# Turning the attention weights of eight more steps by TensorE in a fused top-k attention and feed-forward kernel

## The chip, the cores and the metric

One core of one Trainium2 chip. The metric is the device time of one execution in microseconds (us), as the median of several runs. The engines: TensorE (PE; its weight loads, PEld, overlap it), VectorE (DVE), ScalarE (ACT), GpSimd (POOL) and the queues from which transfers are issued, here nearly all on SyncE (SP). TensorE writes to PSUM, and GpSimd works on SBUF alone in this kernel.

## What is computed

The reference, cut to what matters, with q, k and v of 8 batches x 8 heads x 576 rows x 64, w_in of 512 x 2048 and w_out of 2048 x 512, all float32:

```
scores = scale * np.matmul(q, k.transpose(0, 1, 3, 2))
kth = np.partition(scores, -32, axis=-1)[..., -32:-31]
scores = np.where(scores >= kth, scores, -1000000000.0)
scores = scores - np.max(scores, axis=-1, keepdims=True)
attn = np.exp(scores)
attn = attn / (np.sum(attn, axis=-1, keepdims=True) + 1e-09)
attn_out = np.matmul(attn, v)
x = attn_out.transpose(0, 2, 1, 3).reshape(4608, 512)
h = x @ w_in
return (h - np.tanh(h)) @ w_out
```

## The kernel before

**Steps.** The attention is cut into 144 steps. A step is one pair of heads (hp, four pairs in a batch) and one block of 128 rows (qt); rows 512 to 575 of two pairs of heads make a step of their own (rem). Batch 0 has steps 0 to 17: row blocks 0, 1 and then 2 with 3. Batch 1 has steps 18 to 35: first blocks 0 and 1 of each pair of heads (steps 18 to 25, part a = 0), then blocks 2 and 3 with the two rem steps (26 to 35). Later batches are like batch 1. Two steps of one pair of heads make a pair (nq = 2); the second has `last` set.

**One step on the engines.** TensorE computes the scores of step n+1 while step n is searched (L329), ACT copies them to SBUF (L337). VectorE finds the 32 largest of every row (search, L359 to L382: minima and maxima of quarters, then rounds of MAX8 and MATCH_REPLACE8). GpSimd makes the threshold tb from them (L396), and nb (L405). In the step after, mask (L415 on ACT, L418 on GpSimd) subtracts a huge number from all scores below it, and expo (L438) takes the exponent with its row sum, from which GpSimd makes rd (L448). Two steps after the search, the weights z, 128 rows x 2 heads x 576 keys, are turned so that keys lie on partitions, as the product with v (values, L561) needs them.

**Two ways of turning.** Where the step's flag `pe` is set (in batch 0 alone), turn_pe does it: nine 128x128 transposes on TensorE into PSUM (L533), which ACT copies to et in three pieces (L536). The weights aren't divided by their sum; GpSimd spreads the reciprocals of a pair over 64 columns (spread, L477), TensorE turns these too (L571), ACT copies both results (L575, xs) and GpSimd multiplies them into x (L579). Where `pe` isn't set, VectorE takes the reciprocal of the step (L457), ACT divides the weights by the sum (divide, L464), VectorE turns z in blocks of 32x32 into zx (turn_z, L496; one buffer, of 4 x 576 columns), and after a pair the blocks go to DRAM (there, L509) and back in another order (L513) into et_main or, for rem, et_rem. ACT then copies the product to x (L581).

**Lags.** values of a pair runs `lag` steps after its last step: 2 with pe, 5 (LAG) without.

**The feed-forward.** x of two row blocks of all heads is a unit. Its 30 items are 16 products with w_in (L605; after every second one ACT takes tanh, L631, and a copy, L632, and GpSimd subtracts them, L633) and 14 products with w_out, in the seven products of Strassen's scheme for 2 x 2 blocks, with sums of g by GpSimd (sum_up, L706) and joins (L753). The combinations of w_out that the scheme needs (T1 to T4, 16 of them; combine, L675 to L684) are made by GpSimd once, one with each of the items that follow in steps 17 to 22; two are put aside in DRAM (L681, L686). A dealer (rate and deal in run) hands out items evenly: in every step it takes the smallest rate at which the work at hand lasts until the next unit is ready, which it knows from the steps' lags. A unit of 30 items that is ready at step t moves the rate of all steps before it.

**Order.** All of it is written out by hand, and every engine works in the order of the program. A step n whose step n-2 has pe issues: eight transposes of step n-2 and their two copies, mask of n-1, search of n, spread of n-2 if it is the last of its pair, scores of n+1 with their copy, the ninth transpose and its copy, threshold of n, expo of n-1, most of the dealt items, values of n-2 if it is the last, loads. Without pe, 0.4 of the items are dealt ahead of the scores of n+1; reciprocal, scaling and turning of n-2 stand within the search of n.

**Memory.** `more`, `later` (the tile named spare) and et are areas that serve several purposes in turn: parts of them hold converted weights first, then q of batch 0, rx and xs (the spread reciprocals and the copy of the products), and later T2 to T4. temps, two of the combinations on their way to DRAM, lie in `later`, where et_main is as well. zx1 is first used for weights, later for turn_z.

Of the kernel before, what the change touches and what calls it, by code (L numbers as in the profile page):

```python
# [19 lines left out]
J = 4  # L20
# [34 lines left out]
def kernel(  # L55
# [11 lines left out]
    B, H, S, D = q.shape  # L67
# [3 lines left out]
    R = S - JP  # L71
# [71 lines left out]
    sums = [et_pe[:, 1024 + 512 * i : 1536 + 512 * i].rearrange("p (m n) -> p m n", n=P) for i in range(2)]  # L143
    qT0 = [more[:, i * S : (i + 1) * S] for i in range(4)]
    vb3 = more[:, 2304:2816].rearrange("p (t c d) -> p t c d", t=2, d=D)
    rx2 = [more[:, x : x + 256].rearrange("p (i t d) -> p i t d", i=2, d=D) for x in (2816, 3072)]
    xs0 = more[:, 3328:3840].rearrange("p (a n) -> p a n", a=2)
    q_first = more[:, 3264 : 3264 + S]
    temps = [later[:, i * 512 : (i + 1) * 512].rearrange("p (m n) -> p m n", m=2) for i in range(2)]
    vb_last = later[:, 6 * S : 6 * S + 512].rearrange("p (t c d) -> p t c d", t=2, d=D)  # L150
    kept_B12 = keep.tile([P, CF // 2, 2 * P], FP32, name="kept_B12")
    kept = {x: keep.tile([P, 4, 2 * P], FP32, name=f"kept_{x}") for x in ("T2", "T4")}
# [113 lines left out]
    def load_v(b, hp):  # L266


        if hp == NHP - 1:
            x = vb_last if b else vb3  # L270
        else:
            x = kqpool.tile([P, 2, J, D], FP32, tag="vb", name="vb", bufs=3)[:]
        vb[b, hp] = x
        y = vrs[hp]
        for t in range(2):
            h, o = 2 * hp + t, t * R
            nc.sync.dma_start(
                x[:, t, :, :], v[b, h, o : o + JP, :].rearrange("(c p) d -> p c d", p=P)
            )
            o = 0 if t else JP  # L280
            nc.sync.dma_start(y[half(t), t, :], v[b, h, o : o + R, :])
# [188 lines left out]
    def spread(n):  # L470

        if steps[n].last:
            rd = rds.pop(n)
            nq = steps[n].nq
            last_rx[0] ^= 1
            rx = rxs[n] = rx2[last_rx[0]]
            nc.gpsimd.tensor_copy(  # L477
                rx[:, 0:nq], rd[:, 0:nq].unsqueeze(3).to_broadcast([P, nq, 2, D])
            )
# [38 lines left out]
    def turn_pe(n):  # L518

        g, z = steps[n], st.pop(n)["z"]  # L520
        if g.rem:
            et = et_rem
        elif g.i:
            et = ets.pop(n - 1)
        else:
            et = et_pe
        ets[n] = et
        et = tiles(et, g.nq)[:, :, :, g.i, :].rearrange("p a k j -> p k a j")
        for k0 in range(0, KC, J):
            kn = min(J, KC - k0)  # L530
            zt = zt_ps.tile([P, 512], FP32, tag="zt", name="zt")
            for k in range(kn):
                nc.tensor.transpose(  # L533
                    zt[:, k * P : (k + 1) * P], z[:, (k0 + k) * P : (k0 + k + 1) * P], ident[:]
                )
            nc.scalar.copy(  # L536
                et[:, k0 : k0 + kn],
                zt[:, 0 : kn * P].rearrange("p (k a j) -> p k a j", a=NG, j=G),
            )
            if k0:  # L540
                yield
# [5 lines left out]
    def values(n):  # L547


        g = steps[n]  # L550
        nq, u = g.nq, g.unit
        et = tiles(ets.pop(n), nq)
        w = nq * P
        av = zt_ps.tile([P, 2, N], FP32, tag="zt", name="av")
        for i in range(2 if g.rem else 1):
            cols = half(i) if g.rem else slice(0, w)
            es = et[:, 2 * i : 2 * i + 2] if g.rem else et
            hp = g.hp + i
            for c in range(J + 1):
                for t in range(2):  # L560
                    nc.tensor.matmul(  # L561
                        av[half(t), 0, cols],
                        vb[g.b, hp][:, t, c, :] if c < J else vrs[hp][:, t, :],
                        es[:, :, (J + 1) * t + c if c < J else J].rearrange("p a i j -> p a (i j)"),
                        start=(c == 0),
                        stop=(c == J),
                    )
        if g.pe:
            rx = rxs.pop(n)
            for i in range(nq):  # L570
                nc.tensor.transpose(  # L571
                    in_order(av[:, 1, 0:w], nq)[:, i], rx[:, i].rearrange("p t d -> p (t d)"), ident[:]
                )
            xs = xs0
            nc.scalar.copy(xs[:, :, 0:w], av[:, :, 0:w])  # L575

        def put(dst, order, cols):
            if g.pe:
                nc.gpsimd.tensor_tensor(dst, order(xs[:, 0, cols]), order(xs[:, 1, cols]), ALU.mult)  # L579
            else:  # L580
                nc.scalar.copy(dst, order(av[:, 0, cols]))  # L581

        if g.rem:
            for i in range(2):
                put(xt(u)[:, g.hp + i, g.col : g.col + R], lambda x: x, half(i))
        else:
            dst = xt(u)[:, g.hp, g.col : g.col + w].rearrange("p (i a j) -> p i a j", a=NG, i=nq)
            put(dst, lambda x: in_order(x, nq), slice(0, w))
        if n in done:
            work.extend(ffn(u))  # L590
# [238 lines left out]
    def plan():  # L829
        steps.clear(), done.clear()  # L830

        def block(b, qt):
            return [(slice(0, P), out[b * S + qt * P : b * S + (qt + 1) * P, :])]

        rest = None
        for b in range(B):
            if b % 4 == 0:
                rest = Unit(
                    [
                        [(half(i), out[(b + k + i) * S + JP : (b + k + i + 1) * S, :]) for i in range(2)]  # L840
                        for k in (0, 2)
                    ],
                    "xTr",
                )

            parts = [(0, 1), (2, 3)]
            if b == 0:
                parts[0:1] = [(0,), (1,)]
            for a, qts in enumerate(parts):
                unit = Unit([block(b, qt) for qt in qts], "xT")  # L850
                pe = b == 0
                unit.combines = pe and a == 1
                for hp in range(NHP):
                    for i, qt in enumerate(qts):
                        steps.append(Step(b, hp, qt, unit, 0, i, len(qts), pe, a))
                    if hp == NHP - 1:
                        done[len(steps) - 1] = unit
                    if hp % 2 and a == (0 if b == B - 1 else len(parts) - 1):
                        steps.append(Step(b, hp - 1, J, rest, b % 4 * R, pe=pe, part=a))
                        if hp == NHP - 1 and b % 4 == 3:  # L860
                            done[len(steps) - 1] = rest
        for g, after in zip(steps, steps[1:]):
            if after.pe and not after.rem and not g.pe:
                g.lag = 3
# [4 lines left out]
    def run(exact):  # L869
# [8 lines left out]
        def at(n, fn):  # L878
            todo.setdefault(n, []).append(fn)
# [8 lines left out]
        for n, b, hp, part in sorted(rows):  # L888
# [14 lines left out]
                    at(n - 3 + x, turn)  # L903
                    turned[name] = n - 3 + x
            if not part:
                at(n + 3 if b else n - 1, lambda b=b, hp=hp: load_v(b, hp))

# [191 lines left out]
```

## Time and profile before

| | us |
|---|---|
| runs, median (lowest to highest, 3 runs) | 1490.44 (1490.33 to 1492.73) |
| the profiled execution, its own time | 1491.52 |
| its span, first to last instruction | 1488.7 |
| span until the search of step 20 starts | 226.81 |
| until that of step 28 | 303.33 |
| until that of step 143, the last | 1346.52 |

Busy time, in us, in four stretches of the span (columns: stretch, length, busy time and instructions of PE, PEld, DVE, ACT and POOL, the granted TensorE clock as a share of full speed, the mean busy share of the DMA engines, GB/s):

```profile
0.00:160.00 160.00, 101.50 (x550) 70.51 (x551) 143.88 (x472) 106.27 (x198) 108.42 (x149) 0.84 0.73 239
160.00:303.33 143.33, 128.78 (x1002) 83.44 (x1002) 131.14 (x536) 104.28 (x195) 124.04 (x186) 0.98 0.35 86
303.33:1346.52 1043.19, 1001.83 (x9174) 633.39 (x9172) 1004.16 (x3870) 774.22 (x1427) 808.62 (x1177) 0.99 0.68 174
1346.52:1488.66 142.14, 135.27 (x1254) 89.50 (x1250) 12.80 (x39) 38.37 (x80) 63.74 (x62) 0.98 0.26 74
```

The first stretch loads and converts the weights. In the third, VectorE and TensorE are both above 96% busy. In the last only products are left. A transfer's time to landing and an engine's wait are listed by the profile as "who waited for whom"; a wait for several things is put down to the one that came last.

The rows of the two ways of turning (line, engine, operation, out<-in, shape, count | busy us, mean ns | idle before it, and what ended it):

```profile
L464 ACT ACTIVATE z<-z,rd 128x576 f32<-128x576 f32 x252 | 181.2, 767 | 99.9 <-DVE rd L457 99.3
...
L496 DVE STREAM_TRANSPOSE zx<-z 128x1152 f32<-128x1152 f32 x126 | 171.4, 1361 | 22.8 <-ACT z L464 18.4 <-DMA there<-zx 4.3
...
L533 PE MATMUL zt<-ident,z 128*128 128x128 f32 x162 | 34.0, 351 | 7.6 <-ACT z L438 7.1 <-ACT more L575 0.5
...
L536 ACT COPY et<-zt 128x512 f32<-128x512 f32 x32 | 18.4, 587 | 13.1 <-PE zt L533 12.9
...
L571 PE MATMUL av<-ident,more 128*128 128x128 f32 x18 | 6.1, 374 | 18.2 <-POOL more L477 18.2
```

126 of the steps are turned by VectorE and 18 by TensorE (162 transposes).

### The profile page before, as it was taken

How to read it: one execution, taken by the hardware profiler on the slowest of the kernel's cores; microseconds unless marked ns; L12 is line 12 of the kernel's file. 1: busy time of each engine (PE TensorE's matmuls, PEld its weight loads, DVE VectorE, ACT ScalarE, POOL GpSimd, SP SyncE). 2: the span in 40 equal slices, each digit the busy share in tenths (PEclk: the TensorE clock that was granted, in tenths of full speed). 3: DMA queues.
4: the chain of work that ended last, by engine and by line, in shares of the span. 5: the costliest groups of instructions: out<-in, count | busy, mean ns of one | idle time of the engine just before them, and what ended most of it. 6: DMA issues, size and time to landing. Idle time of an engine off the chain costs nothing.

```text
span 1488.7 us, 34985 instructions
## 1 busy us (share of the span) xinstructions
PE 1367.4 (92%) x11972; PEld 876.8 (59%) x11972; DVE 1292.0 (87%) x4914; ACT 1023.1 (69%) x1898; POOL 1104.8 (74%) x1573
## 2 busy tenths in 40 slices
PE   4667898899989898999999999999999999999998
PEld 2455665556655555656666666666665666656665
DVE  7999898999999999999999999999999999883000
ACT  4767777778677776777687777777777777664321
POOL 3777689968788785968696869696978796866523
PEclk9788999999999999999999999999999999999999
DMA  9955113766767676676766776767676676543311
GB/s 265 377 195 172 39 24 88 186 186 166 182 174 202 149 186 178 173 191 155 180 151 190 175 184 172 188 163 195 165 184 172 173 166 186 153 132 108 102 37 46
DMA packets 257211, 242.24 MB, mean 163 GB/s; under 512 B 193536, under 2 KB 201728, under 8 KB 249856
## 3 DMA queue, kind: packets, MB, share of 16 engines
q1 hardware_dynamic: 255248, 239.69, 60.3%
q8 instruction: 97, 1.59, 0.5%
q14 instruction: 90, 0.74, 0.2%
q10 hardware_dynamic: 1776, 0.22, 0.1%
HBM read 153.99 MB, written 85.85 MB: 161 GB/s over the span
## 4 chain that ended last, share of the span: by engine, by line
PE 49%; DVE 33%; POOL 7%; DMA 6%; ACT 3%; issue 2%; SPq 1%; DVEq 0%; ACTq 0%; POOLq 0%
PE hps L605 19%; PE hx L605 9%; PE hy L605 7%; DVE m L379 6%; PE scps L329 5%; PE av L561 5%; DVE top L371 4%; DVE zx L496 4%; DVE rest L382 4%; DVE ab L365 2%; POOL z L418 2%; DVE top L382 2%; DMA there<-zx 2%; DVE ab L360 2%; POOL g L706 2%
## 5 line engine op out<-in xcount | busy, mean ns | idle before, releaser
L418 POOL TENSOR_TENSOR z<-sc,z 128x576 f32<-128x576 f32 x288 | 405.4, 1430 | 61.2 <-ACT z L415 60.6
L605 PE MATMUL hps<-xT,w_in 128*64 128x256 f32 x3840 | 436.2, 383 | 5.4 <-ACT g L632 5.1
L605 PEld LDWEIGHTS hps<-xT,w_in 128*64 128x64 f32 x3840 | 271.7, 138 | 163.6 <-issue 23.7
L633 POOL TENSOR_TENSOR g<-g,th 128x512 f32<-128x512 f32 x144 | 184.2, 1280 | 113.3 <-ACT g L632 112.1
L464 ACT ACTIVATE z<-z,rd 128x576 f32<-128x576 f32 x252 | 181.2, 767 | 99.9 <-DVE rd L457 99.3
L438 ACT ACTIVATE z<-z,nb 128x576 f32<-128x576 f32 x288 | 221.9, 776 | 15.2 <-POOL z L418 15.2
L415 ACT ACTIVATE z<-sc,tb 128x576 f32<-128x576 f32 x288 | 208.2, 775 | 31.8 <-POOL tb L396 25.6
L329 PE MATMUL scps<-kT,qT 64*128 64x288 f32 (+1 forms) x1120 | 161.0, 438 | 39.4 <-DVE top L367 33.2
L371 DVE MAX8 top<-ab 128x8 f32<-128x144 f32 x864 | 194.4, 293 | 0.0
L337 ACT COPY sc<-scps 128x1152 f32<-128x1152 f32 x144 | 160.8, 1117 | 46.2 <-PE scps L329 45.5
L496 DVE STREAM_TRANSPOSE zx<-z 128x1152 f32<-128x1152 f32 x126 | 171.4, 1361 | 22.8 <-ACT z L464 18.4
L379 DVE MAX8 m<-rest 128x8 f32<-128x168 f32 x576 | 161.1, 320 | 0.0
L379 DVE MAX8 m<-top 128x8 f32<-128x144 f32 (+1 forms) x576 | 152.2, 305 | 0.0
L329 PEld LDWEIGHTS scps<-kT,qT 64*128 64x128 f32 (+1 forms) x1120 | 88.4, 180 | 97.6 <-ACT z L415 33.9
L631 ACT ACTIVATE th<-hps 128x512 f32<-128x512 f32 x144 | 84.4, 586 | 73.1 <-PE hps L605 67.0
L605 PE MATMUL hx<-w_out,g 128*64 128x256 f32 x1088 | 131.8, 392 | 1.6 <-POOL g L633 1.6
L605 PE MATMUL hy<-more,g 128*64 128x256 f32 x1088 | 125.3, 380 | 0.0
L396 POOL TENSOR_SCALAR tb<-m 128x1 f32<-128x1 f32 x288 | 84.3, 302 | 35.9 <-DVE m L379 35.2
L605 PEld LDWEIGHTS hx<-w_out,g 128*64 128x64 f32 x1088 | 78.2, 141 | 49.9 <-issue 6.3
L365 DVE TENSOR_TENSOR ab<-scps,sc 128x576 f32<-128x576 f32 x144 | 107.5, 746 | 0.0
L605 PEld LDWEIGHTS hy<-more,g 128*64 128x64 f32 x1088 | 76.8, 137 | 42.9 <-issue 5.4
L422 POOL TENSOR_SCALAR bad<-top,tb 128x3 uint8<-128x3 f32 x288 | 96.6, 343 | 0.2
(118 smaller groups left out, 2324.1 us busy)
## 6 DMA issues: line engine op xcount, KB each, us to landing
there<-zx SPq DMA_DIRECT2D x56, 1152.0 KB, 4.7
spare<-there SPq DMA_DIRECT2D x224, 288.0 KB, 5.2
more<-kept_T SPq DMA_DIRECT2D x34, 512.0 KB, 3.9
kin<-in_k_dram SPq DMA_DIRECT2D x116, 72.0 KB, 4.2
out_dram<-ot SPq DMA_DIRECT2D x32, 256.0 KB, 2.8
there<-zx SPq DMA_DIRECT2D x14, 576.0 KB, 7.2
spare<-there SPq DMA_DIRECT2D x56, 144.0 KB, 3.0
vb<-in_v_dram SPq DMA_DIRECT2D x48, 128.0 KB, 4.9
```

Source lines behind the costliest of these rows:

```text
L329: nc.tensor.matmul(ps[rows, t, s, 0:S2], qT[g.b, g.hp + i, g.part][half(t), qs], kT[g.b, g.hp + i][half(t), ks], start=True, stop=True,)
L337: nc.scalar.copy(sc[:], ps[:, :, :, 0:S2])
L365: nc.vector.tensor_tensor(low[:, :, :, 0:W2], thirds(near), thirds(far), ALU.min)
L371: nc.vector.max(top[:, t, o : o + 8], low[:, t, i, :])
L379: nc.vector.max(m[:, t, m8], seen[i][t])
L415: nc.scalar.activation(zv[:, t, :], scf[:, t, :], AF.Relu, bias=tb[:, t : t + 1], scale=-BIG)
L418: nc.gpsimd.tensor_tensor(zv[:, t, :], scf[:, t, :], zv[:, t, :], ALU.subtract)
L438: nc.scalar.activation(x["zv"][:, t, :], x["zv"][:, t, :], AF.Exp, bias=x["nb"][:, t : t + 1], scale=scale, accum_out=den[:, t : t + 1],)
L464: nc.scalar.activation(x, x, AF.Copy, scale=rds[n][:, g.i, t : t + 1])
L496: nc.vector.transpose(tiles(zx, g.nq)[:, :, :, g.i, :].rearrange("p c k j -> p k c j"), z[:].rearrange("p (k c j) -> p k c j", c=NG, j=G),)
L605: nc.tensor.matmul(acc[half(t)], lhs[:, half(t)], rhs, start=start, stop=stop, skip_group_check=True)
L633: nc.gpsimd.tensor_tensor(g, g, th[:], ALU.subtract)
```

## The change

Steps 18 to 25, the first part of batch 1, get `pe`, and so turn_pe, spread and the multiplication by GpSimd in place of reciprocals, scaling, turn_z and the way through DRAM. With the flag their lag becomes 2. The last hunk but one holds `combines` and the rem steps to batch 0. The other edits give these steps their places in memory: et_main as et, a second pair of rx and a second xs in et_rem, and temps in zx1. The loads of v for batch 1 are issued one step before its pair and not three steps after.

```
-    rx2 = [more[:, x : x + 256].rearrange("p (i t d) -> p i t d", i=2, d=D) for x in (2816, 3072)]
-    xs0 = more[:, 3328:3840].rearrange("p (a n) -> p a n", a=2)
+    rxs2, xss = [], []
+    for y in (more[:, 2816:3840], et_rem[:, 0:1024]):
+        rxs2.append([y[:, x : x + 256].rearrange("p (i t d) -> p i t d", i=2, d=D) for x in (0, 256)])
+        xss.append(y[:, 512:1024].rearrange("p (a n) -> p a n", a=2))
...
-    temps = [later[:, i * 512 : (i + 1) * 512].rearrange("p (m n) -> p m n", m=2) for i in range(2)]
+    temps = [zx1[:, i * 512 : (i + 1) * 512].rearrange("p (m n) -> p m n", m=2) for i in range(2)]
...
-            rx = rxs[n] = rx2[last_rx[0]]
+            rx = rxs[n] = rxs2[steps[n].b][last_rx[0]]
...
         else:
-            et = et_pe
+            et = et_main if g.b else et_pe
...
-            xs = xs0
+            xs = xss[g.b]
...
-                pe = b == 0
-                unit.combines = pe and a == 1
+                pe = b == 0 or (b == 1 and a == 0)
+                unit.combines = b == 0 and a == 1
...
-                        steps.append(Step(b, hp - 1, J, rest, b % 4 * R, pe=pe, part=a))
+                        steps.append(Step(b, hp - 1, J, rest, b % 4 * R, pe=b == 0, part=a))
...
-                at(n + 3 if b else n - 1, lambda b=b, hp=hp: load_v(b, hp))
+                at(n + 3 if b > 1 else n - 1, lambda b=b, hp=hp: load_v(b, hp))
```

## The prediction

> **What bounds the kernel now.** I read the page first: which engine is full, and where.
>
> ```profile
> PE 1367.4 (92%) x11972; PEld 876.8 (59%) x11972; DVE 1292.0 (87%) x4914; ACT 1023.1 (69%) x1898; POOL 1104.8 (74%) x1573
> ...
> DVE  7999898999999999999999999999999999883000
> ...
> POOL 3777689968788785968696869696978796866523
> ```
>
> VectorE is full from start to 1346 us, then TensorE alone works off the last products (142 us to the end). So the change pays only if the search of some step starts earlier and stays earlier. Number the steps from 0, and call S(n) the time at which VectorE starts the search of step n (its first L359). The change touches steps 18 to 25, whose turning falls two steps later, in steps 20 to 27. In slices 6 to 8 (186 to 298 us) POOL stands at 8, 9, 9, 6 of ten, its highest of the run, and not VectorE alone. So I asked next for busy times in stretches that begin at S(19), S(20) and so on to S(29) (columns: stretch, its length, busy PE, PEld, DVE, ACT, POOL, granted clock, DMA share, GB/s).
>
> ```profile
> 217.74:226.81 9.07, 8.51 (x60) 5.16 (x61) 7.97 (x35) 6.36 (x14) 8.70 (x14) 1.00 0.17 43
> 226.81:236.14 9.33, 9.33 (x111) 6.29 (x109) 8.84 (x35) 8.01 (x16) 9.17 (x15) 1.00 0.20 34
> 236.14:248.14 12.00, 9.20 (x80) 5.34 (x75) 9.19 (x34) 8.01 (x16) 11.84 (x16) 1.00 0.13 33
> 248.14:259.80 11.66, 8.22 (x56) 4.81 (x56) 8.84 (x36) 7.39 (x13) 11.50 (x15) 0.85 0.55 178
> 259.80:268.24 8.44, 5.98 (x38) 3.73 (x40) 8.41 (x35) 5.14 (x8) 8.28 (x11) 0.80 0.80 184
> ...
> 294.89:303.33 8.44, 6.41 (x58) 3.99 (x55) 8.40 (x35) 5.67 (x10) 6.88 (x14) 1.00 0.53 128
> 303.33:311.77 8.44, 7.53 (x66) 4.48 (x62) 8.40 (x35) 5.95 (x11) 5.13 (x9) 1.00 0.75 207
> ```
>
> The two long steps, 21 and 22 (12.00 and 11.66 us), are POOL's: 11.84 and 11.50 us busy, because the 16 combinations of w_out and the sums of g fall here. From S(23) on a step is as long as VectorE's work (8.40 of 8.44). POOL's own list shows one gap (0.69 us) between 225 and 301 us; it stands back to back until then, and only after 301 us does it wait. The waits of VectorE between 217.74 and 303.33 us are few:
>
> ```profile
> DVE rd L457 <- POOL rd L448: 3.2, 2, 2.8
> DVE zx L496 <- DMA there<-zx: 2.8, 1, 2.8
> DVE scps L359 <- ACT sc L337: 0.9, 2, 0.5
> ```
>
> **What VectorE loses.** Eight stream transposes (L496, 1361 ns) and four of eight reciprocals (L457, 147 ns): 10.9 + 0.6 = 11.5 us. The one wait for zx (2.8 us, in step 22) goes too. VectorE's busy time in steps 20 to 27 is 8.84, 9.19, 8.84, 8.41, 8.89, 8.40, 8.79, 8.40, in sum 69.8; without 11.5 it is 58.3, 7.3 a step. If nothing else bound, S(28) would come at 226.81 + 58.3 = 285.1 and not at 303.33: 18.2 us earlier. That is the most that can be won.
>
> **What is hidden anyway.** The four round trips through DRAM (issued on SP's queue: one there and four spare issues a pair) and the sixteen scalings on ACT (L464, 767 ns, 12.3 us) go. ACT gets instead eight times 587 + 587 + 271 ns of copies (11.6 us) and four copies of av (586 ns) for four of xT (370 ns): even, and ACT has 5.1 to 8.0 of 8.4 to 12 us busy. The four issues that load v for a pair (two L277, two L281) move from three steps after its first step to one step before it, ahead of four steps' loads of q and k on SP. SP is held there in any case (21.3 us in two waits of L686 for POOL's L684). The buffers are free by then: their last readers, values of steps 12 to 17, run in steps 14 to 19, and the loads stand in steps 17 to 23. The data are read from step 21 on, four steps after the first load. Worth nothing either way; were the cover gone, a landing (4.9 us) would show once. The products' temporary moves from later to zx1, which is idle until step 28.
>
> **What TensorE gets.** Nine transposes a step: eight take 0.97 us start to start in the steps of batch 0, the ninth 0.17, so 8 x 1.14 = 9.1 us, and 4 x 0.27 for the turned reciprocals. It also has no later place to go: lag falls from 5 to 2, so values of a pair runs inside the stretch (2.2 us a pair), and the dealer must finish the unit before batch 1 by step 28 and not 30, which worked through by its rule gives three products in every one of steps 19 to 28 (30) where it gave 27. A product is 1.75 us (16 records). From the end of the scores of step 20 (224.81) to those of step 29: 27 products 47.3, 1 to 2 more in step 28 (2.6), values 1.3 + 4 x 2.47 = 11.2, transposes 9.3, scores 9 x 1.17 = 10.5, in sum 81: 305.8, and S(29) one copy (1.1 us) later, 306.9, against 311.77. TensorE alone would allow a gain of 4.9 us.
>
> The skill has a rule that speaks against this part. In the stretch 160 to 240 us, where batch 0's steps run the same transposes, the granted clock is 1.00 with TensorE 97 to 99.6% busy (19.35 to 19.92 of 20 us). The Trainium skill, "TensorE: Matmul & The Clock Gate", Part 4: PE-mode transpose, says that transposes don't count as activity for the clock gate and puts one at about 275 ns in a kernel. By that the nine would take 2.5 us, an estimate from the page, and the change would lose 10.7 us more on TensorE; the trace's 0.97 us for eight decides.
>
> **What POOL gets.** For each pair a spread of the reciprocals (L477, 0.38 us start to start) and a multiplication (L579, 0.71), nothing goes. Its chain can be summed, as it has no gap. Between one step's tb (L396) and the next lie a fixed 4.56 us (z 2.77, bad 0.60, tb 0.54, nb 0.34, rd 0.31), 1.235 for each 128x512 operation, 0.71 for a join. Check on the kernel before, from tb of step 19 (228.84) to that of step 26: 7 x 4.56 + 26 x 1.235 + 0.62 + 0.71 = 65.4, so 294.2; the trace has 295.08 with its gap of 0.69. After: 27 operations (the dealer is one product ahead), three spreads and three multiplications more, 69.9 us: tb(26) at 298.7, z of step 25 done at 298.1. That is 3.6 us later than now.
>
> **How they join.** In such a step, each engine in its order, the search of step n+3 follows z of step n thus: exponent 1.3, transposes 1.0, their copies 0.6, two relus 1.4, scores' copy 1.1, with small waits for a copy of av or a tanh ahead on ACT 0.3 to 1.2: 5.7 to 6.6 us. So S(28) = 298.1 + 5.7 to 6.6 = 303.8 to 304.7, against 303.33. In step 28 the order changes back: after the transposes of step 25 (done 300.5) TensorE has scores 1.2, the ninth 0.2, three products 5.3, values 2.5, then one or two products ahead of the scores of step 29 (1.75 to 3.5), scores and copy 2.3: S(29) = 313.6 to 315.3 against 311.77, +1.8 to +3.5; VectorE by itself gives 304.2 + 8.44 = 312.7, +0.9. What is won until S(23) (about 255.5 by the same chain, 4 us early) is thus paid back by S(28). I take **+2.5 us**, nearer the upper end as TensorE and POOL are both full there. From S(29) on, steps are VectorE's again, so the shift stays to the end. The profiled execution took 1491.5 (span 1488.7), 1.1 above the median of the runs, so 1490.4 + 2.5 = **1492.9**; its own range, from -1 (POOL's chain shorter by one product of the dealer's and its wait) to +4.5 (one more such wait), is 1489.4 to 1494.9.
>
> **Rivals.** (B) POOL's place in the order isn't binding: the steps turned by TensorE need POOL's sum in every second step only (the 3.2 us of waits of L457), TensorE sets the pace, and S(29) comes 4.9 us early: 1485.5; with VectorE setting it, 18.2 early: 1472.2, which needs a TensorE that keeps up at 7.3 us a step with 8.9 us of work, so hardly. For it: the gaps ACT leaves; against it: POOL's gapless list. (C) Slower, through one wait: TensorE meets the spread of the reciprocals (L571 on L477) with nothing behind it in its queue that could run.
>
> ```profile
> PE av L571 <- POOL more L477: 18.2, 9, 3.1
> ```
>
> That is 2.0 us a time in batch 0. With POOL a step behind, four pairs give 8.1 us, of which the chain above holds 0.7: 1490.4 + 2.5 + 7.4 = 1500.3. It decides from the point where POOL's tb comes over 2 us after TensorE has finished values. (D) The change gives only part of what it says: the first trip of step 27's pair meets a late SP queue again, 2.8 us in step 30 and not in 22, on top of the +2.5: 1495.7.
>
> **Chances.** A, the forecast 0.50; B 0.25; C 0.18; D 0.07. About 0.2% (3 us) is what a measurement of this kernel can tell from no change. Within A two fifths lie over +3 us, so slower is 0.20 + 0.17 + 0.05 = 0.42, faster 0.24 (B but for its edge), same 0.34. The range takes in B's 4.9 us with 1 us for its error, and C to where three of its four waits show: 1484.5 to 1498.5; B's far end (0.05) and the rest of C (0.1) are left out.
>
> **What would show it.** S(23) earlier by some 4 us, but S(28) within 2 us of 303.33: the joined chain. POOL without gaps from 228.8 to 299 with tb(26) near 298.7: POOL's sum. Transposes of eight at 0.97 and a clock of 1.00 between 226 and 300 us: TensorE's price. L571's waits on L477 at over 8 us in the four new pairs: C. I am wrong if S(30) lies more than 3 us before 320.60, or if the steps after it have another length than now.

## The result and the profile after

The changed kernel takes 1498.16 us (median of six runs, 1496.57 to 1499.72) against 1490.64 us for the kernel before in the same session (six runs, 1490.33 to 1492.73). The ratio is 1.005 with a 95% interval of 1.004 to 1.006: slower by 0.5%, some 7.5 us. The forecast was 1492.9, so the result lies 5.3 us above it, above the forecast's own range and just inside the wide one.

Line numbers after the change are two higher than before (the spread L477 is now L479, its reader L571 is L573, POOL's z L418 is L420). First the engine totals and slices of the page, changed kernel.

```profile
PE 1374.5 (92%) x12052; PEld 883.3 (59%) x12052; DVE 1282.7 (86%) x4902; ACT 1021.9 (68%) x1906; POOL 1109.0 (74%) x1581
...
DVE  7998897799999999999999999999999999883000
...
POOL 3777689978778686868686869696878787775533
```

VectorE has 12 instructions fewer and a little less to do, and its slices 7 and 8 (224 to 299 us, counted from 1) are now 7, not 8 and 9: it stands idle there, in the very steps that were to get faster. From slice 9 on it is full as before.

The profiled execution took 1498.62 us, span 1496.6 (before 1491.52 and 1488.7), so the span grew by 7.9 us. Splitting both spans at the start of the search of the same step n, S(n), and at the last matmul shows where this arises (last matmul: its start; one profile of each kernel):

| part of the span | before, us | after, us | difference |
|---|---|---|---|
| start to S(18) | 210.20 | 211.30 | +1.1 |
| S(18) to S(29), the steps changed | 101.57 | 107.05 | **+5.5** |
| S(29) to S(143) | 1034.75 | 1032.30 | -2.4 |
| S(143) to the last matmul | 135.26 | 135.27 | 0.0 |
| last matmul to the end | 6.88 | 10.68 | **+3.8** |

The second row is the one that the forecast put at +2.5. It is taken apart next with the stretches from S(20) to S(29) of the changed kernel (columns as in the prediction: stretch, length, busy PE, PEld, DVE, ACT, POOL, granted clock, DMA share, GB/s).

```profile
227.90:237.21 9.31, 9.31 (x108) 6.41 (x106) 7.52 (x33) 6.58 (x14) 9.15 (x15) 1.00 0.22 38
237.21:246.03 8.82, 8.82 (x79) 5.72 (x77) 7.92 (x33) 7.29 (x15) 8.43 (x12) 1.00 0.00 1
246.03:259.38 13.35, 11.06 (x81) 6.78 (x79) 7.58 (x33) 6.72 (x13) 13.19 (x18) 0.87 0.30 85
259.38:268.33 8.95, 8.77 (x77) 5.67 (x75) 7.33 (x32) 7.15 (x15) 8.65 (x13) 1.00 0.14 43
268.33:280.46 12.13, 9.67 (x83) 6.02 (x81) 7.68 (x32) 6.77 (x14) 10.26 (x15) 1.00 0.19 38
280.46:289.62 9.16, 8.01 (x69) 4.95 (x67) 7.24 (x32) 6.55 (x14) 8.78 (x12) 1.00 0.12 20
289.62:300.08 10.46, 10.46 (x91) 6.59 (x89) 7.67 (x33) 6.16 (x13) 10.30 (x16) 1.00 0.21 61
300.08:307.86 7.78, 7.78 (x69) 5.04 (x67) 7.33 (x32) 5.84 (x13) 4.58 (x9) 1.00 0.06 9
307.86:318.35 10.49, 10.49 (x94) 6.47 (x92) 8.62 (x34) 6.88 (x14) 9.16 (x17) 1.00 0.12 39
```

The rows are steps 20 to 28. VectorE needs 7.2 to 7.9 us in each of steps 20 to 27, and only step 27 is that short. In steps 20, 21, 26, 27 and 28 the first busy number equals the length: TensorE sets the step. In step 22 POOL does (13.19 of 13.35). Step 24 is the odd one: 12.13 us long and **no** engine full, TensorE 9.67, POOL 10.26. Something waits there in a ring, one engine for another and back. The list of waits of the changed kernel between 218 and 318 us names its parts (columns: who waits for whom, total us, times, longest).

```profile
ACT z L440 <- POOL z L420: 13.8, 16, 3.4
DVE scps L361 <- ACT sc L339: 10.5, 7, 2.7
DVE top L369 <- POOL bad L424: 9.9, 6, 3.4
...
POOL z L420 <- ACT z L417: 5.0, 3, 3.1
...
PE av L573 <- POOL spare L479: 4.7, 2, 2.5
```

VectorE's idle time is the second and third row, 20.4 us. The kernel before had 0.9 us of the first of these two kinds up to 303 us and none of the second. The last row is rival C's wait, in two of the four new pairs (in the stretches of steps 22 and 24). The second of them on the timeline, TensorE first, then POOL (start, us, what, and in brackets the idle time before it and its releaser):

```profile
271.01 0.60 PE L563 MATMUL av<-spare,vr 128*64 128x256 f32 x4
274.07 0.44 PE L573 MATMUL av<-ident,spare 128*128 128x128 f32 x2 [2.46 <-POOL spare L479]
274.44 1.95 PE L607 MATMUL hps<-xT,w_in 128*64 128x256 f32 x16
276.32 1.09 PE L535 MATMUL zt<-ident,z 128*128 128x128 f32 x8
```

```profile
270.28 2.76 POOL L420 TENSOR_TENSOR z<-sc,z 128x576 f32<-128x576 f32 x2
273.05 0.63 POOL L424 TENSOR_SCALAR bad<-top,tb 128x3 uint8<-128x3 f32 x2
273.63 0.39 POOL L479 COPY spare<-rd 128x256 f32<-128x256 f32 x1
...
278.84 2.79 POOL L420 TENSOR_TENSOR z<-sc,z 128x576 f32<-128x576 f32 x2 [1.69 <-ACT z L417]
```

TensorE has finished values at 271.6 us and needs the spread reciprocals; POOL makes them at 273.63, behind z (2.76) and bad. TensorE runs nothing between 271.6 and 274.07: the product at 274.44 and the eight transposes at 276.32 stand behind the wait, though no wait of their own shows. The transposes' late end then makes ACT's copies and its relu (L417) late, and POOL, which was to be without gaps, stands 1.69 us at 278.84 waiting for that relu. POOL made TensorE wait, and TensorE made POOL wait, in one step. That is how step 24 gets long with no engine full.

The same wait in step 22 (2.29 us, up to 251.42) did something else. 1.4 us after it the granted clock fell to half for 3.4 us, from 252.8 us on:

```profile
251.42 0.44 PE L573 MATMUL av<-ident,spare 128*128 128x128 f32 x2 [2.29 <-POOL spare L479]
251.79 2.69 PE L607 MATMUL hps<-xT,w_in 128*64 128x256 f32 x16
254.41 1.97 PE L535 MATMUL zt<-ident,z 128*128 128x128 f32 x8
```

A product of 16 records takes 2.69 us here and 1.95 at 274.44, eight transposes 1.97 against 1.09: 1.6 us more on TensorE, and the 0.87 in the stretch's row is this.

The last row of the table, the end, is not on any engine's busy list. Per window it is idle time only (from 15.3 us before the last matmul to the end; before in the first fence, after in the second):

```profile
1466.52:1488.70 22.18, 15.42 (x144) 10.00 (x140) 0.15 (x1) 1.86 (x5) 3.44 (x5) 0.89 0.22 76
```

```profile
1470.65:1496.60 25.95, 15.43 (x144) 10.00 (x140) 0.15 (x1) 1.86 (x5) 3.43 (x5) 0.84 0.19 65
```

Every engine's work is equal to 0.01 us and only the length differs, by 3.77. The trace's records of the sequencers tell what stands there. After the last output each engine takes the branch past the recomputation for ties and runs a short closing list of semaphore instructions. Times in us after the last matmul:

```
          SP branch   first semaphore   second   third    last
before      1.80           4.95          5.05     5.14    6.82
after       1.81           5.31          5.41     8.91   10.62
```

In both kernels every engine stands 3.1 to 4.5 us behind its branch. In the changed kernel SP stands once more, 3.5 us between two neighbouring semaphore instructions, and the other engines wait for SP. The second of the two names a semaphore that was last raised 0.6 us after the last matmul, at the landing of an output, so nothing that it waits for is outstanding.

Code that has still to arrive would explain both stands. The trace has transfers on the instruction queues here, in two rounds in either kernel: from 2.1 us on, just after the branches, and from 5.2 us on (before) or 5.6 us on (after). SP stops at 5.41 us, just ahead of the second round, and goes on at 8.91 us, some 3 us after the last transfer of that round began (5.91). The kernel before is through its list at 6.82 us without a stop. That fits, but it doesn't show that SP waits for this round. The next packet on these queues tells nothing: it starts at 9.56 us in the kernel after, when SP has gone on, and at 8.41 us in the kernel before, behind its end.

The change removes 24 of SP's records (1346 before, 1322 after; 20 of them are transfers), so its closing list lies elsewhere. Whether the place of the code is the cause is the first experiment.

### The profile page after: what moved, and what is told of

Its sections match the earlier page's. It is cut to its first block, busy times and chain, and to the rows that moved or that the text cites. A ratio compares the mean times of both kernels' runs of the same rounds, so it can differ in the third digit from the quotient of the medians.

```text
span 1496.6 us, 35125 instructions
## 1 busy us (share of the span) xinstructions
PE 1374.5 (92%) x12052; PEld 883.3 (59%) x12052; DVE 1282.7 (86%) x4902; ACT 1021.9 (68%) x1906; POOL 1109.0 (74%) x1581
## 4 chain that ended last, share of the span: by engine, by line
PE 49%; DVE 33%; POOL 8%; DMA 4%; ACT 3%; issue 2%; SPq 1%; DVEq 0%; ACTq 0%; POOLq 0%
PE hps L607 19%; PE hx L607 9%; PE hy L607 7%; DVE m L381 6%; PE scps L331 5%; PE av L563 5%; DVE top L373 5%; DVE rest L384 4%; DVE zx L498 4%; POOL z L420 3%; DVE ab L367 2%; DVE top L384 2%; DVE ab L362 2%; POOL g L708 2%; DVE scps L361 1%
## 5 line engine op out<-in xcount | busy, mean ns | idle before, releaser
L420 POOL TENSOR_TENSOR z<-sc,z 128x576 f32<-128x576 f32 x288 | 405.4, 1429 | 58.9 <-ACT z L417 58.4
L607 PEld LDWEIGHTS hps<-xT,w_in 128*64 128x64 f32 x3840 | 269.9, 137 | 158.2 <-issue 20.4
L466 ACT ACTIVATE z<-z,rd 128x576 f32<-128x576 f32 x236 | 169.6, 767 | 98.5 <-DVE rd L459 98.1
L417 ACT ACTIVATE z<-sc,tb 128x576 f32<-128x576 f32 x288 | 208.4, 776 | 23.1 <-POOL tb L398 19.0
L331 PE MATMUL scps<-kT,qT 64*128 64x288 f32 (+1 forms) x1120 | 157.9, 429 | 30.9 <-DVE top L369 29.5
L498 DVE STREAM_TRANSPOSE zx<-z 128x1152 f32<-128x1152 f32 x118 | 160.7, 1362 | 20.8 <-ACT z L466 19.2
L361 DVE TENSOR_TENSOR scps<-scps,sc 128x288 f32<-128x288 f32 x144 | 63.8, 443 | 38.7 <-ACT sc L339 38.5
```

What stands on the lines that cost most here:

```text
L331: nc.tensor.matmul(ps[rows, t, s, 0:S2], qT[g.b, g.hp + i, g.part][half(t), qs], kT[g.b, g.hp + i][half(t), ks], start=True, stop=True,)
L417: nc.scalar.activation(zv[:, t, :], scf[:, t, :], AF.Relu, bias=tb[:, t : t + 1], scale=-BIG)
L420: nc.gpsimd.tensor_tensor(zv[:, t, :], scf[:, t, :], zv[:, t, :], ALU.subtract)
L466: nc.scalar.activation(x, x, AF.Copy, scale=rds[n][:, g.i, t : t + 1])
L498: nc.vector.transpose(tiles(zx, g.nq)[:, :, :, g.i, :].rearrange("p c k j -> p k c j"), z[:].rearrange("p (k c j) -> p k c j", c=NG, j=G),)
L607: nc.tensor.matmul(acc[half(t)], lhs[:, half(t)], rhs, start=start, stop=stop, skip_group_check=True)
```

## The experiments

Theory at the start: of the 7.9 us, 3.8 are a stop for code at the end; in the changed steps POOL's sum and TensorE's list hold each other up, and the waits on the spread are where it shows. Rivals: the wait alone is the loss (take it away and the steps are as forecast); TensorE's three products a step are the loss; POOL's sum alone is. All runs are told here; "stretch" is S(18) to S(29), 101.57 us before and 107.05 after, "end" is last matmul to the end.

**e1: the code's position.** Twelve transfers are put into the branch that never runs. Nothing that runs is different (each engine has as many records as in the kernel after), and SP's code is longer by these transfers and their semaphore instructions.

```
             with tc.If(again > 0):
+                for _ in range(3):
+                    bring_corners()
...
```

> The changed kernel with 12 more transfers in the branch that is never run (the second, exact pass), so that the code behind the branch lies further on; nothing that runs is altered. Theory: of the 7.9 us by which the span of the changed kernel is longer, 3.8 lie behind the last matmul, where SP stands still for 3.5 us between two closing semaphore instructions while one more block of instructions is fetched; which block the closing code falls into depends on the length of the code before it. Then the time from the last matmul to the end falls from 10.5 to about 6.8 us, the start of the search of step 28 stays near 307.9, and the time is about 3.7 us less than the changed kernel's 1498.2, so 1494.5. Rival: the 3.8 us are the changed kernel's own (a transfer still under way, or chance from run to run): the end stays at 10.5 us, or varies without regard to the code, and the time stays at 1498.

Measured: the end is 7.21 us and not 10.68, and SP's first three records come at 5.29, 5.39 and 5.47 us, without a stop. The median is 1494.66 against 1491.87 (ratio 1.0015, 1.0006 to 1.0025). So about half of the 0.5% was where a piece of code lies: 3.5 of the 7.5 us by the ends, more by the ratios. But the stretch, with the same running code, is 108.75 us, 1.7 more than after's. The timeline of TensorE in e1 says why:

```profile
274.49 0.44 PE L573 MATMUL av<-ident,spare 128*128 128x128 f32 x2 [2.45 <-POOL spare L479]
274.86 3.31 PE L607 MATMUL hps<-xT,w_in 128*64 128x256 f32 x16
```

The wait is the same 2.45 us as after's 2.46, but here half clock follows it (from 275.3, for 3.4 us) and the product takes 3.31 and not 1.95. The same wait has this consequence in one profile and not in the other, so a single profile of this stretch can be 1.7 us off by it. The Trainium skill, "TensorE: Matmul & The Clock Gate", Part 1, says that the activity is judged in free-running windows of about 3.4 us; lengths of 3.4, 6.8 and 10.2 us in these traces agree, and so does the same wait with and without a consequence. The same page's advice in "Why this matters for your kernels", no idle gaps above about 3 us between bursts of matmuls, is too generous for these traces: half clock followed waits of 2.29 and 2.45 us.

**e2: the spread ahead of the mask.** In the new steps spread(n-2) is emitted before mask(n-1), so POOL makes it before z and bad.

```
-            if here(-1):
+            early = pe and steps[n - 2].b == 1
+            if here(-1) and not early:
                 mask(n - 1, exact)
...
+            if early:
+                mask(n - 1, exact)
```

> The changed kernel with GpSimd's spread of the reciprocals (L479) ahead of the masking of the next step (L420) in the eight steps. Theory: TensorE stands 2.3 and 2.5 us at the turning of the reciprocals (L573) behind the masking, with a product behind it, and in step 23 this delays the transposes, their copies, the relu and so GpSimd's next masking by 1.7 us. Without it the waits of L573 on L479 go from 4.7 to under 1 us, and the search of step 28 starts 2 us earlier (near 305.9 where now 307.9). Rival: the sum of GpSimd's work sets the stretch whatever the order: the waits of L573 go, and step 28 stays within 0.5 us of 307.9.

Measured: stretch 106.14, only 0.9 shorter, where the theory expected 2 us and the rival at most 0.5; median 1498.2 against 1491.87 (1.0037, 1.0023 to 1.005). The wait on the spread is gone from TensorE's list, but others stand in its place (waits of e2, 218 to 314 us):

```profile
ACT z L440 <- POOL z L420: 17.5, 16, 3.9
DVE top L369 <- POOL bad L424: 13.5, 6, 3.9
...
PE zt L535 <- ACT z L440: 1.9, 2, 1.2
...
PE zt L535 <- ACT spare L577: 1.7, 2, 1.2
```

TensorE now waits 3.6 us ahead of its transposes, and VectorE waits 13.5 us for POOL's bad where it waited 9.9. Its idle time as a whole is 19.7 us and was 20.4: it moves from one kind to the other. The masking, now behind the spread, starts later by the spread's 0.4 us. POOL's gap ahead of z, 1.69 us in step 24 of the kernel after, is 0.53 us here, and tb of step 24 comes 0.9 us earlier after S(18): that is the whole gain.

```profile
278.73 2.79 POOL L420 TENSOR_TENSOR z<-sc,z 128x576 f32<-128x576 f32 x2 [0.53 <-ACT z L417]
```

So taking this wait away is worth 0.9 us, not 2, and the wait taken by itself is not the loss.

**e3: POOL relieved.** The two combinations T2 and T4 of each group of w_out go from POOL to VectorE.

```
-            nc.gpsimd.tensor_tensor(t2, b22, b12, ALU.subtract)
+            nc.vector.tensor_tensor(t2, b22, b12, ALU.subtract)
...
-            nc.gpsimd.tensor_tensor(t4, b21, t2, ALU.subtract)
+            nc.vector.tensor_tensor(t4, b21, t2, ALU.subtract)
```

> The changed kernel with the eight combinations T2 and T4 of w_out (L681, L686) on VectorE in place of GpSimd. Theory: GpSimd's sum sets steps 20 to 24 of the changed kernel, so taking eight times 1.235 = 9.9 us off it lets the steps run at TensorE's pace: the search of step 29 starts between 307 and 311 where now 318.4 (before: 311.8), and VectorE has room, as it is busy 7.3 to 7.9 us in steps of 8.8 to 13.4. Rival: TensorE's work sets the stretch alone (products, values and transposes in sum 81 us): step 29 stays within 1.5 us of 318.4. Second rival: VectorE's eight operations (some 0.65 us each) wait in its order for data and delay the searches: step 29 later than 318.4.

Measured: stretch 102.17, 4.9 shorter; S(29) at 312.16, 1.2 us later than the latest that was expected of POOL's theory. Median 1490.57 against 1491.87 (0.9989, 0.9977 to 1.0): the whole loss is gone, though not by the stretch alone. Of the span's 7.5 us against after's, 4.9 are the stretch, 3.3 the end (7.35), 1.3 the time before S(18); 2.0 go back after S(29). POOL's waits in 218 to 314 us, e3:

```profile
ACT z L440 <- POOL z L420: 9.3, 14, 1.6
...
DVE top L369 <- POOL bad L424: 1.1, 2, 0.6
```

VectorE's 9.9 us of waiting for bad fall to 1.1. What it pays is seen in its first stretches (e3):

```profile
226.60:238.10 11.50, 11.50 (x128) 7.86 (x126) 10.61 (x35) 7.14 (x15) 11.34 (x16) 1.00 0.30 63
238.10:248.44 10.34, 9.54 (x82) 6.00 (x79) 10.25 (x37) 7.92 (x17) 9.93 (x12) 1.00 0.17 55
```

VectorE is at 10.61 and 10.25 us in steps 20 and 21 where after had 7.52 and 7.92. That is more than the operations moved there need by themselves. Two of them on VectorE, and what POOL does beside the second:

```profile
245.42 0.67 DVE L686 TENSOR_TENSOR zx<-w_out,et 128x512 f32<-128x512 f32 x1
...
247.31 1.21 DVE L686 TENSOR_TENSOR more<-w_out,more 128x512 f32<-128x512 f32 x1
```

```profile
244.02 3.95 POOL L420 TENSOR_TENSOR z<-sc,z 128x576 f32<-128x576 f32 x2
```

Two operations of one kind and size take 0.67 us and 1.21 us. Five of the eight take 0.67 to 0.69 us, the others 1.21, 1.79 and 1.88. Beside them four of POOL's operations take 1.73 to 2.57 us (of the two z above the first 1.42, the second 2.57), where in before and after no single one in the stretch takes over 1.5 us. So the two engines hold each other up here too, and the move costs more than its list. S(23) comes no earlier; all of the 4.9 us is between S(23) and S(29) (53.83 against 58.97). POOL's sum is thus a large part of the loss. A part of the 4.9 us may be the clock: e3 has no half clock in the stretch, where after has 3.4 us of it.

**e4: fewer products in the stretch.** The dealer may finish the new unit two steps later, so fewer products are dealt up to step 28. The trace has 26 between the scores of step 20 and those of step 29, where after has 28: two fewer, not the three expected.

```
-                    ready[g.unit] = m + g.lag + g.pe
+                    ready[g.unit] = m + g.lag + g.pe + 2 * (g.pe and g.b == 1)
```

> The changed kernel with the dealer told that the first unit of batch 1 is ready two steps later than it is, so that it deals 27 and not 30 products in steps 19 to 28, as in the kernel before. Theory that both TensorE and GpSimd set the stretch: three products of 1.75 us fewer on TensorE, hardly less on GpSimd (one operation of 1.235 us): the search of step 29 starts 1 to 3 us earlier than 318.4, and the products put off are made up in steps 29 to 38. If TensorE sets it alone: 4 to 5 us earlier. If GpSimd alone: within 1.3 us of 318.4.

Measured: stretch 105.48, 1.6 shorter; median 1497.84 (1.0038, 1.0026 to 1.0049). Two products are 3.5 us of TensorE's time, and less than half of that comes out: TensorE is a part of the ring, not the bound by itself. A wait for the spread of 4.2 us, with 6.8 us of half clock from 0.4 us before its end, fell in this stretch as well (after has 3.4 us), so 1.6 is likelier too small than too large.

```profile
270.94 0.69 PE L573 MATMUL av<-ident,spare 128*128 128x128 f32 x2 [4.20 <-POOL spare L479]
```

**e5: the control.** The kernel before, with T2 and T4 on VectorE as in e3.

> The kernel before, with the eight combinations T2 and T4 on VectorE in place of GpSimd, as in the run of the changed kernel that did the same and won 4.9 us between the searches of steps 18 and 29 (102.2 us where the changed kernel takes 107.1 and the kernel before 101.6). Theory: without the change VectorE is full there (69.8 us busy in the 76.5 us of steps 20 to 27), so eight operations of 0.65 us on it cost what GpSimd gains: steps 18 to 29 take 100 to 103 us, no more than 1.5 us off 101.6. With the change VectorE had the room. Rival: moving the combinations is worth 4 to 5 us by itself: 96.5 to 97.5 us.

Measured: stretch 103.25, 1.7 **longer** than before's and just over the 103 expected, median 1491.93 against 1492.41 (0.9998, 0.9989 to 1.0007). Its stretches for steps 20 and 21:

```profile
225.81:237.36 11.55, 11.55 (x131) 7.58 (x127) 11.48 (x36) 9.54 (x19) 11.39 (x17) 1.00 0.16 28
237.36:249.71 12.35, 8.44 (x58) 4.94 (x56) 12.06 (x38) 8.62 (x16) 12.00 (x18) 0.86 0.24 78
```

VectorE is at 11.48 of 11.55 and 12.06 of 12.35: in the kernel before there is no room on it for these combinations. Here too some of them are drawn out (1.43 to 1.78 us for three of the eight), and the stretch has 17 us of half clock where before has 6.8, so the 1.7 us is not the price of the list alone. So e3's gain is not one that could be had without the change; it is what the change frees on VectorE, put to use.

**e6, e7: the cures together.** e6 is the changed kernel with the edits of e2, e3 and e4, e7 with those of e3 and e4 alone.

> The changed kernel with all three alterations: T2 and T4 on VectorE, the spread ahead of the masking, and 27 products dealt in steps 19 to 28 and not 30. Theory that GpSimd's sum and TensorE's sum set the stretch together: with both lightened, VectorE's saving of 11.5 us comes through in part: steps 18 to 29 take 97 to 100 us (kernel before 101.6), and the time is 2 to 4 us under that of the kernel before if no further block of code is fetched at the end, 1 us over to 1 us under if it is. Rival: the changed steps cost TensorE, ACT and GpSimd a chain of waits that none of this shortens: 102 us or more.

> The same without the spread's move: T2 and T4 on VectorE, and 27 products. If the spread's place matters once GpSimd is lightened, steps 18 to 29 take 1 us more than with it; if GpSimd is no longer behind, the waits of TensorE for the spread (0.5 us in the run with the combinations alone moved) are gone anyway and the two agree within 0.5 us. Theory: the second, 97 to 100 us.

Measured: stretches 97.76 and 97.73 us, medians 1488.58 and 1487.71 against 1492.41 (0.9973, 0.9961 to 0.9985, and 0.9967, 0.9955 to 0.998). Both beat both kernels, by more than was expected of a kernel with a second stop at its end, which both have (1 us over to 1 us under). Together e3 and e4 give 9.3 us where each alone gave 4.9 and 1.6: with one of the two engines relieved the other can be next, so that the sum of the single gains is too low. How much of this is the clock is open: e3, e6, e7 and e8 have no half clock in the stretch, after has 3.4 us and e4 6.8. If half of each window is lost, an estimate from above, the single gains would be 3.2 and 3.3 and the two together 7.6. And e2's order is worth nothing once POOL has time. Steps 23 to 25 of e7:

```profile
258.46:265.64 7.18, 5.95 (x51) 3.96 (x51) 7.15 (x34) 4.57 (x8) 7.02 (x9) 1.00 0.43 102
265.64:273.16 7.52, 7.28 (x61) 4.59 (x59) 7.49 (x33) 6.21 (x12) 6.34 (x12) 1.00 0.01 2
273.16:281.04 7.88, 7.88 (x69) 5.13 (x67) 7.20 (x33) 6.80 (x15) 6.62 (x11) 1.00 0.13 22
```

7.18 with VectorE at 7.15, 7.52 with VectorE at 7.49: here, for two steps, VectorE sets the pace of a step turned by TensorE. That is what the change could give.

**e8: the best, with the code shifted.** e7 with e1's twelve transfers.

> The changed kernel with T2 and T4 on VectorE and 27 products dealt, plus the 12 transfers in the branch that is never run. Theory: the two gains are apart and add up: steps 18 to 29 take 97.7 us as without the transfers, and the time from the last matmul to the end falls from 9.6 to about 7 us, so 2.5 us less than 1487.7: 1484.5 to 1486, some 6 us under the kernel before. Rival: the end depends on something else than where its code lies, and stays at 9.6 us: 1487.7.

Measured: 1486.35 against 1492.13 (0.9963, 0.9949 to 0.9977), the fastest of all; but the end is 9.31 us and not 7, so the expectation was missed, and of the 2.2 us by which its span is shorter than e7's 2.0 lie before S(18) (209.84 against 211.80), where nothing differs. The sequencers' records show why the shift did not help. In e7 and e8, as in e6, SP no longer stops by itself; POOL does, and SP waits for POOL (us after the last matmul):

```
      SP, in the closing list      POOL, in the closing list
e1    no stop                      no stop                      end  7.21
e3    no stop                      no stop                      end  7.35
e4    5.53 to 8.68                 no stop                      end 10.45
e7    no stop                      5.17 to 8.62                 end  9.58
e8    no stop                      6.63 to 8.63                 end  9.31
```

e3 takes nine records from POOL and gives VectorE eight; SP has one more (1323), and yet SP's stop is gone in e3. So a shift that moved the stop out of the way in one kernel says nothing of the next. Which lengths give a second stop, and on which engine, stays open. The seven profiles with a second stop have one thing in common: the engine that stopped goes on at 8.5 to 8.9 us, whether it stopped at 5.0 or, as in e8, at 6.6, and each time a second round of instruction transfers had begun at 5.4 to 6.0 us. The profiles without a second stop have such a round too. That fits a stop for code, and isn't shown to be one.

**e9: the changed kernel once more,** unchanged, beside e8.

> The changed kernel as it is, once more, to tell what of its profile repeats. Theory: steps 18 to 29 take 107 us within 2 us (half-clock windows of TensorE fall differently), and the end 10.3 to 10.7 us after the last matmul. The 1.1 us of steps 9 and 10 are chance: between -1 and +2 us against the kernel before. Rival: the end varies from run to run between 7 and 10.7 us.

Measured: 1498.11 against 1492.13 (1.0042, 1.0027 to 1.0057), stretch 107.04, end 10.30, and S(18) at 209.49, 0.7 *before* the kernel before's. The stretch and the end repeat; the +1.1 before S(18) does not, so it isn't the change's.

| | stretch | end | ratio to before |
|---|---|---|---|
| before | 101.57 | 6.88 | |
| after, and again | 107.05, 107.04 | 10.68, 10.30 | 1.005, 1.0042 |
| e1 code shifted | 108.75 | 7.21 | 1.0015 |
| e2 spread first | 106.14 | 10.29 | 1.0037 |
| e3 T2, T4 to VectorE | 102.17 | 7.35 | 0.9989 |
| e4 fewer products | 105.48 | 10.45 | 1.0038 |
| e5 before with e3's edit | 103.25 | 6.91 | 0.9998 |
| e6 e2 + e3 + e4 | 97.76 | 9.65 | 0.9973 |
| e7 e3 + e4 | 97.73 | 9.58 | 0.9967 |
| e8 e7, code shifted | 97.74 | 9.31 | 0.9963 |

## Why the prediction was right or wrong

**VectorE's 11.5 us.** The instructions went (118 stream transposes, not 126). VectorE's busy time in steps 20 to 27 fell from 69.8 to 60.3, by 9.5. The durations of VectorE's rows in before's 76.5 us add up to over 81 us: in the records an instruction begins before the one ahead ends, so taking some out frees less than their durations. The term was 2 us too large. It did not matter: all of it became idle time, as VectorE did not set the end.

**What was costed at nothing.** Right for the round trips, ACT and the loads: the waits between 218 and 318 us name no DMA, and ACT is at 5.8 to 7.3 us a step. Rival D did not come: step 30 (S(30) to S(31)) takes 8.44 us in both kernels, and the 2.8 us wait for zx does not return up to there.

**TensorE.** Transposes of eight 1.0 to 1.1 us and a clock of 1.00 but for one window: right. The forecast's estimate from the page took the duration of one transpose for its share of the time: a record lasts 0.30 us here, but the next starts 0.11 us after it. Three products a step: right, and e4 tells what two fewer give, 1.6 us.

**POOL's sum.** Allowing for the 1.09 us by which the profile after was late at S(20), tb of steps 20 to 23 comes at 238.92, 250.26, 261.68 and 272.93 against 238.96, 250.1, 261.5 and 272.6 by the forecast's prices for what POOL has in each step (the record has only their end, tb(26)): within 0.35 us for four steps, through a wait of TensorE of 2.29 us and a window of half clock. Then tb(24) is at 281.15, 2.05 late by the same sum, and tb(26) at 300.93, not 298.7. The gap of 1.69 us at 278.84 accounts for most of it. "POOL without gaps" held to 277 us, but for 0.2 us here and there, and then failed. (A slip of reading that changes nothing: slices 6 to 8 of POOL's row are 8, 9, 9, the 6 is the ninth, and single nines stand further on too.)

**The join: the step that failed.** Less the same offset, S(28) comes at 306.77 and was put at 303.8 to 304.7; S(29) comes at 317.26 and not at 313.6 to 315.3 (the terms as written give 0.2 more than that). The order behind it was right: 6.4 us from the end of z of step 25 to S(28) by the same chain (5.7 to 6.6 predicted), and 10.49 from S(28) to S(29) (9.8 to 10.6). What failed is the sum of POOL taken as if it waited for no one, and TensorE's wait for the spread, of which the chain held 0.7 us for all four pairs. Two pairs had it, 2.29 and 2.46 us, 4.7 in all, and the second came back to POOL as the gap. With both engines over 90% full in these steps (84.4 and 82.5 of 90.5 us) each passed its delay to the other. That is rival C's wait at a little over half of its size, though e2 gives only 0.9 us for taking it away, and C's point of decision, "POOL's tb over 2 us after TensorE has finished values", is what the timeline shows: values end at 271.6, tb starts at 274.02.

**S(23) four microseconds early** was wrong, 0.4 before and not 4 (1.5 with the offset): step 22 was 13.35 us, with POOL at 13.19 and half clock on TensorE. POOL's tb was on time and the chain from it to the search was longer. Rival B (TensorE alone sets the pace, S(29) 4.9 us early) fell: S(29) came late. TensorE sets five of the nine steps, POOL the longest. e3 gave 4.9 us and e4 1.6, but e3 takes 9.9 us off POOL and e4 3.5 off TensorE, with different windows of half clock, so which engine weighs more is not shown.

**"The shift stays to the end"** was half right. The steps from 30 on have before's lengths (S(30) to S(49) 165.83 against 165.81 us). But between S(49) and S(70) the changed kernel wins 2.1 us back. There TensorE falls to half clock two or three times; the two runs with three windows of 6.8 us (before, e3) take 187.2 and 186.7 us from S(49) to S(70), and the nine with windows of 13.6 us in all take 185.1 to 185.8. That this goes with the windows is seen in eleven profiles; why an earlier shift changes them was not tried.

**The end.** Nothing in the prediction spoke of it, and it is half of the loss in the span. e1 shows it for the changed kernel: 3.5 us less with not one running instruction different. From the page of before it could not have been summed; what could have been said is that the change shortens SP's list by 24 records, that each engine already stands over 3 us after its last branch, and that its closing code could come to lie differently. That the time still lies in the wide range, which was drawn for rivals B and C, is in part luck: 3.8 us at the end and -2.4 us after S(29) are in it, and neither was forecast.

So the stretch was read from the right place (POOL's sum, joined with TensorE) and at half of its size; the end was not read at all; and what comes back after S(49) hides some of both. How the stretch's missing 3 us divide between the waits and the half clock stays open: e2 takes the waits for the spread away and gains 0.9, while relieving both engines gains 9.3 and has no half clock.

## What to carry to other kernels

When work moves from an engine that is full to two that are over 90% full in the same stretch, adding up each engine's list gives a lower bound only: look for pairs of instructions with which the two wait for each other inside one step, and charge each such wait on both. The freed engine's room is worth something only if work is handed on to it: here eight operations given to VectorE and two products dealt later turned 0.5% slower into 0.3% faster, and the two edits gave more together than the sum of each, with some of the difference perhaps the clock's. For differences of a few microseconds, split the span at landmarks (the first changed step, the last one, the last matmul) before explaining anything, since a code position alone moved this kernel by 3.5 us.

## What the runs showed of the hardware

An engine can stop twice at the end without a wait that the trace shows. Behind the last branch every engine stands 3.1 to 4.6 us, and in seven of eleven profiles SP (3.0 to 3.5 us) or POOL (2.0 to 3.7 us) stands a second time. The end takes 6.9 to 7.4 us without the second stop and 9.3 to 10.7 with it. That the place of the code is behind it is shown by e1 alone, where only code that never runs was added; that the engine waits for code to arrive is not shown.

A wait of TensorE of 2.3 to 2.5 us for the spread, among dense matmuls, was followed after 0.8 to 1.4 us by a window of half clock of 3.4 us in three cases (after and e9 in step 22, e1 in step 24), and by none in three others (after and e9 in step 24, e1 in step 22). Over all eleven profiles, between 160 and 1346 us, TensorE has 60 waits of 1.8 to 2.6 us; 15 were followed within 1.6 us by half clock, the shortest of them 1.82 us long. Within a profile the windows' starts lie a multiple of 3.41 us apart. The time before S(18) also differs, by up to 2.9 us, between kernels whose code is nearly the same there (S(18) 209.21 to 212.09); the half clock up to S(18) does not explain it by itself, as e1 and e8 have as much of it (54.6 us) and lie 1.8 us apart.

VectorE and POOL can hold each other up. An operation on two 128x512 tensors took VectorE 0.67 to 0.69 us in five cases and 1.21 to 1.88 in three, and beside those three one of POOL's maskings took up to 2.57 us and 1.4 otherwise (e3).
